# A product-gradient ring, an earlier load list and a skewed first group in the tail of an adaLN / spectral / GLU backward kernel

## The chip, the cores and the metric

The kernel runs on one core of a Trainium2 chip. The metric is device time of one execution in microseconds (us); a set of runs is given by its median, lowest and highest. A profiled execution has a time of its own and a span, from the first recorded instruction to the last. The engines are TensorE (PE, matrix products; its weight loads are PEld), VectorE (DVE), ScalarE (ACT), GpSimd (POOL) and SyncE (SP, here used only to issue DMA transfers; POOL issues some too). PE runs at a granted clock which the profile shows as a share of full speed (PEclk).

## The reference

A block of a diffusion transformer, forward and backward. The forward part, cut to what matters (S = 2048, D = 576, F = 4608, bf16):

```python
mod = (silu(c) @ w_mod).reshape(1, 6, 1, -1)
sa, ca, ga, sb, cb, gb = (mod[:, k] for k in range(6))
h = layernorm(x) * (1 + ca) + sa
x = x + ga * irfft2(rfft2(h) * (w_r + 1j * w_i))
h = layernorm(x) * (1 + cb) + sb
x = x + gb * (((h @ w_gate) * (h @ w_up)) @ w_down)
```

The function returns x and, for a given grad_out, the gradients of x, w_r, w_i, w_gate, w_up, w_down, c and w_mod: out_0 to out_8. The Fourier transforms are done as matrix products with tables. Three outputs matter here. out_0 is the forward result, whose last product is h @ w_down, the "down projection". out_8, the gradient of w_mod [576, 3456], is an outer product: for each of the six sections of 576 columns (one for each of sa, ca, ga, sb, cb, gb), silu(c) as a column times the section's gradient as a row. out_7, the gradient of c, needs for each of the 576 rows of w_mod the sum over all columns of w_mod times the same gradients.

## The kernel before, in words

The kernel computes the gradients of the GLU first, in stages that fill most of the span. The part that the change touches is its tail, from L976, the last 285 us or so. It has two kinds of work for PE.

One is three staged pipelines over the 16 row tiles (128 rows each) or 8 pairs of columns. Stage 1 (t1_norm, t1_out, t1_turn, t1_last) is the backward pass of the second layer norm and the first transform along the columns; its tile gx is written to DRAM by POOL (L1223, one store for each tile t). Stage 2 (t2_cols, t2_rows, t2_filter, t2_back) goes through the spectral filter; its products b_GY, fm, sd are made by DVE and used by PE, sd at L256. Stage 3 (t3_cols, t3_rows, t3_norm, t3_sums) transforms back and ends with the first layer norm; its result ob is out_1.

The other is the down projection (L1471 to L1515), which fills PE's gaps in those pipelines. It goes over 8 pairs of row tiles (tp_). A pair's hidden values come in four tiles named hl (quarters of 9 blocks of 128, L1293), and w_down, in blocks of 128 rows, lies in six tiles named wd, loaded once (L1279): blocks from 0, 7, 14, 21 and 28 on, seven each, and block 35. For each row tile ti of the pair and half h of the columns there is a group of NFB = 36 matmuls (L1495) into one PSUM bank u3p; there are two such banks, and in the last pair banks u3q besides. In the first pair the two row tiles of one half are done together, block by block, so that both banks run side by side. When a bank is full, ACT copies it (ob, L1500), which frees the bank; with both halves there, DVE multiplies and adds twice (of, L1508 and L1509; for the last tile in halves, L1512 and L1513) and POOL stores the tile (L1514).

The order on each engine is written out by hand. `deal` (L1055) puts 24, 24 and 21 matmuls of the down projection into each step of the three stages, and fixes the order of PE, ACT and DVE; `in_order(end_sp)` fixes SP's queue at the end; `behind` puts a transfer behind a given instruction. POOL's order comes from the list at L1309: each entry names a tile t of stage 1 and the loads that are issued directly behind the store of its gx, an integer being an hl quarter and a pair (f0, n) a wd tile.

```python
for t, *loads in ((1, (0, 7)), (2, 0), (3, (7, 7)), (4, 1), (5, (14, 7)), (6, 2), (7, (21, 7), 3), (8, (28, 7), (35, 1))):
```

The six buffers of hl tiles lie in six pools, and a table at L1293 says which tile goes into which.

out_8 is made by `product_rows` (L1147): for section j and row block m (five: four of 128 rows and one of 64), ACT scales the gradient row d by silu(c) (L1152) into one slice of a tile o8 [128, 5, 576]. There is one buffer of it. With the fifth block SP issues two stores, one of four blocks (L1154) and one of the last 64 rows (L1155). Four sections (their gradients lie in the tile early) are done in stage 2, two row blocks in each of its steps, the last two (gradients in the tile ends: dca for ca, MCA, and dsar for sa, MSA) after stage 3.

The sums for out_7 are made by `section_sum` (L1161): DVE multiplies a tile of w_mod with the gradients, writes the products into a scratch tile pr and adds them up into a column of gsc, a tile that a POOL memset (L1028) has set to zero. Row blocks of the first four sections are read into tiles wmE (three buffers, so that blocks 3 and 4 are loaded again into the first two when their sums are done), the last two into wmL (four buffers, block 4 being loaded again). After the sums come gs, gcf, gcd (L1548 to L1552), two matmuls gcp (L1558), gcr and the store of out_7.

At the end SP issues, in this order: hl loads of the last pair, four loads of wmL, two stores of a part of the filter gradient (gback_d, L1523), the stores of the rows of MCA, the reloads wmE 3 and 4 (L1159), two copies in DRAM that reverse that part into out_2 and out_3 (L1539), the rows of MSA, the last wmL, out_7.

add_zero (L1102) opens the PSUM banks in which column sums grow (csA to csE), by a product of the identity with a tile of zeros.

Of the kernel before, what the change touches and what calls it, by code (L numbers as in the profile page):

```python
# [86 lines left out]
def build(ctx, tc, A_x, A_w_r, A_w_i, B_w_gate, B_w_up, B_w_down, c_in, w_mod, grad_out,  # L87
# [58 lines left out]
    def traced():  # L146
        return len(nc.cur_bb.bb.instructions)
# [828 lines left out]
    with ExitStack() as ts:  # L976
# [11 lines left out]
        tl0 = pool("tl0", 1)  # L988
        zero = tl0.tile([128, 512], BF, name="zero")
        tl = pool("tl", 1)  # L990
# [111 lines left out]
        def add_zero(*banks):  # L1102

            for cs in banks:
                nc.tensor.matmul(cs[:], lhsT=ident[:], rhs=zero[:], start=True, stop=False)

# [37 lines left out]

        o8s = {}

        def product_rows(j, m, d):  # L1147

            if m == 0:
                o8s[j] = tl.tile([128, 5, D], BF, name="o8")  # L1150
            r, o8 = RM[m], o8s[j]
            nc.scalar.activation(out=o8[r, m, :], in_=d[r, :], func=ACT.Copy, scale=sc_col[r, m:m + 1])  # L1152
            if m == 4:
                nc.sync.dma_start(out_8[0:512, j * D:(j + 1) * D].rearrange("(m q) n -> q m n", q=128), o8[:, 0:4, :])  # L1154
                nc.sync.dma_start(out_8[512:576, j * D:(j + 1) * D], o8[64:128, 4, :])  # L1155

# [4 lines left out]
        def section_sum(m, wm, d, n, k):  # L1161
            r = RM[m]
            return nc.vector.scalar_tensor_tensor(out=pr[r, 0:n * D], in0=wm[r, :], scalar=1.0, in1=d[r].rearrange("p j n -> p (j n)"), op0=MUL, op1=MUL, accum_out=gsc[r, m, k:k + 1])

# [123 lines left out]
        def hl_load(nq, eng=nc.sync, behind_=None):  # L1288
            if nq >= 28:
                hl = hlp.tile([128, 9, 256], BF, name="hl2")  # L1290
            else:
                slot[0] += 1
                hl = hlt[(0, 3, 2, 4, 1)[slot[0]] if slot[0] < 5 else (0, 3, 2, 5, 4, 1)[(slot[0] + 1) % 6]].tile([128, 9, 256], BF, name="hl")  # L1293
            queued(eng, behind_, hl[:], hhT_d[nq // 4, :, 9 * (nq % 4):9 * (nq % 4) + 9, :])
            if nq == 13:
                in_order([last[eng], ld3["gxc", "ins", 0]])
            return hl
# [10 lines left out]
        first_hl = []  # L1308
        for t, *loads in ((1, (0, 7)), (2, 0), (3, (7, 7)), (4, 1), (5, (14, 7)), (6, 2), (7, (21, 7), 3), (8, (28, 7), (35, 1))):  # L1309
            for x in loads:  # L1310
                if isinstance(x, int):
                    first_hl.append(queued_load(t, hl_load, x, nc.gpsimd))
                else:
                    queued_load(t, wd_load, *x)
# [148 lines left out]
        wme = [secp.tile([128, 4 * D], BF, name="wmE%d" % k) for k in range(3)]  # L1463
        pr = secp.tile([128, 4 * D], BF, name="pr")
        secq = pool("secq", 1, "right", stack=rA)
# [6 lines left out]
        for tp_ in range(NT // 2):  # L1472
# [10 lines left out]
            for group in [[(0, 0), (1, 0)], [(0, 1), (1, 1)]] if tp_ == 0 else [[(0, 0)], [(0, 1)], [(1, 0)], [(1, 1)]]:  # L1483
                mark = traced()
                p2 = {}
                for ti, h in group:
                    n3 = 4 * tp_ + 2 * ti + h
                    p2[ti] = ps_cs.tile([128, 512], FP32, name="u3q", tag="cs" + "AB"[n3 // 2 % 2]) if tp_ == NT // 2 - 1 and n3 % 2 else ps_u3.tile([128, 512], FP32, name="u3p")
                    if h == 0:
                        obs[ti] = o2p.tile([128, D], BF, name="ob3", bufs=4)  # L1490
                for fb in range(NFB):
                    f0, w = wd_part(fb)
                    mms = []
                    for ti, h in group:
                        mm = nc.tensor.matmul(p2[ti][:, 0:288], lhsT=hls[fb // 9][:, fb % 9, ti * 128:(ti + 1) * 128], rhs=w[:, fb - f0, h * 288:(h + 1) * 288], start=(fb == 0), stop=(fb == NFB - 1))  # L1495
                        mms.append(mm)
                for (ti, h), mm in zip(group, mms):
                    if (tp_, ti, h) == (NT // 2 - 1, 1, 1):
                        continue
                    followed(mm, nc.scalar.copy(obs[ti][:, h * 288:(h + 1) * 288], p2[ti][:, 0:288]))  # L1500
                proj += pe_since(mark)
                for ti, h in group:
                    if h == 0:
                        continue
                    t = 2 * tp_ + ti
                    of = o2p.tile([128, D], BF, name="of3", bufs=3)
                    if t < NT - 1:
# [6 lines left out]
                    nc.gpsimd.dma_start(o0_v[:, t, :], of[:])  # L1514
                then_dve[mms[-1].ins.name] = of_engine(mark, "DVE")  # L1515
        end_sp += [i_ for i_ in nc.cur_bb.bb.instructions[last_mark:] if i_.engine == mybir.EngineType.SP]
        end_pe = []
        with tc.issue_after(ld3["last"]):
# [3 lines left out]
            for c in range(2):  # L1522
                nc.sync.dma_start(gback_d[c], wn[:, c, NPR + 1:NT, 0:DF])  # L1523
            end_sp += of_engine(mark_sp, "SP")
            for at, (j, d) in zip((12, 12), ((MCA, dca), (MSA, dsar))):
                mark_pe = traced()
                spread(d)
                for m in range(5):
                    product_rows(j, m, d)
                end_pe.append((at, pe_since(mark_pe), of_engine(mark_pe, "Activation")))  # L1530
            mark = traced()
            for m in range(5):
                section_sum(m, wmE[m][0], early, 4, 0)
                if m < 2:
                    wmE.append(section_load(m + 3, MGA, 4, wme[m]))
                    end_sp.append(wmE[-1][1])
            mark_sp = traced()
            for c, o_v in enumerate((o2_v, o3_v)):
# [86 lines left out]
```

## Time and profile before

| | |
|---|---|
| three runs | 1529.7 us median, 1525.87 to 1531.91 |
| the profiled execution | 1528.03 us, its span 1526.3 us |
| mean granted clock of TensorE | 0.985 |
| busy: PEld | 987.9 us, 65% of the span |
| busy: DVE | 1047.6 us, 69% |
| busy: ACT | 559.5 us, 37% |
| busy: POOL | 233.1 us, 15% |

How to read it: a busy time is the sum over an engine's instructions, without those that only issue a transfer or wait. In a row of a timeline stand the start and the length in us, the engine, the line of the kernel, the operation, what is written and read (out<-in), shapes, how many instructions are taken together (x), and in brackets the idle time of the engine just before it with what ended it. "DMA wd<-..." there is the landing of a transfer. An instruction of SPq or POOL named DMA_DIRECT2D is the issue of a transfer; the landing comes later. The DMA share is the mean busy share of the 16 DMA engines.

### The profile page before, as it was taken

How to read it: one execution, taken by the hardware profiler on the slowest of the kernel's cores; microseconds unless marked ns; L12 is line 12 of the kernel's file. 1: busy time of each engine (PE TensorE's matmuls, PEld its weight loads, DVE VectorE, ACT ScalarE, POOL GpSimd, SP SyncE). 2: the span in 40 equal slices, each digit the busy share in tenths (PEclk: the TensorE clock that was granted, in tenths of full speed). 3: DMA queues.
4: the chain of work that ended last, by engine and by line, in shares of the span. 5: the costliest groups of instructions: out<-in, count | busy, mean ns of one | idle time of the engine just before them, and what ended most of it. 6: DMA issues, size and time to landing. Idle time of an engine off the chain costs nothing. (4 is left out here: it accounts for less than half of the span.)

```text
span 1526.3 us, 27836 instructions
## 1 busy us (share of the span) xinstructions
PE 1460.6 (96%) x10713; PEld 987.9 (65%) x10713; DVE 1047.6 (69%) x2537; ACT 559.5 (37%) x1196; POOL 233.1 (15%) x370
## 2 busy tenths in 40 slices
PE   7999999999999999999999999999999997999965
PEld 5665544666766666667666666676666675777653
DVE  7485755676766767767666777676676675497974
ACT  7566833222222222222222222222222265475541
POOL 1101211110111111112011011021110122202210
PEclk8999999999999999999999999999999999999997
DMA  9967975868776876866777687687685678836884
GB/s 336 303 192 215 241 222 157 175 137 167 171 152 126 172 150 138 156 147 152 146 154 158 132 162 162 119 172 149 132 178 111 133 208 312 286 121 186 228 245 100
DMA packets 486836, 271.12 MB, mean 178 GB/s; under 512 B 409677, under 2 KB 456910, under 8 KB 486318
## 3 DMA queue, kind: packets, MB, share of 16 engines
q1 hardware_dynamic: 459454, 170.15, 51.7%
q0 software_dynamic: 27248, 99.18, 21.9%
q8 instruction: 84, 1.38, 0.4%
q14 instruction: 50, 0.41, 0.1%
HBM read 105.14 MB, written 81.25 MB: 122 GB/s over the span
## 5 line engine op out<-in xcount | busy, mean ns | idle before, releaser
L914 DVE TENSOR_TENSOR acc<-acc,u8p 128x288 f32<-128x288 f32 (+1 forms) x1088 | 482.4, 452 | 276.7 <-PE u8p L909 272.8
L909 PE MATMUL u8p<-wT,ggT 128*128 128x288 bf16 x1152 | 327.9, 286 | 1.5 <-DVE acc L914 1.4
L909 PE MATMUL u8p<-wT,guT 128*128 128x288 bf16 x1152 | 327.6, 286 | 0.0
L870 PE MATMUL gup<-h2T,wgu 128*128 128x512 bf16 x1152 | 297.8, 379 | 0.0
L789 ACT CAST so<-u57p 128x288 bf16<-128x288 f32 x208 | 83.0, 399 | 507.2 <-PE u57p L787 507.2
L1495 PE MATMUL u3p<-wd,hl 128*128 128x288 bf16 x1080 | 152.8, 291 | 32.4 <-ACT ob L1500 22.6
L787 PE MATMUL u57p<-h2p,gg_sf 128*128 128x288 bf16 x1088 | 176.6, 286 | 0.0
L787 PE MATMUL u57p<-h2p,gu_sf 128*128 128x288 bf16 x1088 | 176.6, 286 | 0.0
L870 PEld LDWEIGHTS <-wgu 128*128 128x128 bf16 x1152 | 109.6, 98 | 97.9 <-issue 17.1
L909 PEld LDWEIGHTS <-ggT 128*128 128x128 bf16 x1152 | 112.6, 98 | 66.4 <-issue 14.0
L578 PE MATMUL u4p<-goT,wdT 128*128 128x512 bf16 x668 | 154.6, 379 | 0.8 <-ACT ghh_st L172 0.8
L1495 PEld LDWEIGHTS <-hl 128*128 128x128 bf16 x1152 | 112.6, 99 | 64.9 <-issue 32.2
L909 PEld LDWEIGHTS <-guT 128*128 128x128 bf16 x1152 | 112.7, 98 | 57.1 <-issue 2.0
L872 ACT CAST gT<-gup 128x512 bf16<-128x512 f32 x144 | 84.4, 586 | 131.4 <-PE gup L870 129.5
L787 PEld LDWEIGHTS <-hh_sf 128*128 128x128 bf16 x1152 | 112.7, 98 | 28.4
L787 PEld LDWEIGHTS <-gu_sf 128*128 128x128 bf16 x1088 | 106.5, 98 | 27.0
L787 PEld LDWEIGHTS <-gg_sf 128*128 128x128 bf16 x1088 | 106.5, 98 | 26.8
L872 ACT CAST uT<-gup 128x512 bf16<-128x512 f32 x144 | 84.4, 586 | 77.8 <-PE gup L870 77.0
L578 PEld LDWEIGHTS <-wdT 128*128 128x128 bf16 x668 | 63.6, 98 | 72.2 <-issue 6.5
L787 PE MATMUL u57p<-gonC,hh_sf 128*128 128x288 bf16 x576 | 99.7, 286 | 0.0
L885 POOL DMA_DIRECT2D hhT_d<-hhT x36 | 33.2, 923 | 373.4 <-DVE hhT L874 372.8
L172 ACT CAST ghh_st<-u4p 128x512 bf16<-128x512 f32 x102 | 58.4, 586 | 59.6 <-PE u4p L578 57.5
(270 smaller groups left out, 1694.2 us busy)
## 6 DMA issues: line engine op xcount, KB each, us to landing
hhT_d<-hhT POOLq DMA_DIRECT2D x36, 512.0 KB, 6.5
ghhT_d<-ghh_st POOLq DMA_DIRECT2D x35, 512.0 KB, 3.6
ghh<-ghhT_d POOLq DMA_DIRECT2D x35, 512.0 KB, 7.5
hl<-hhT_d SPq DMA_DIRECT2D x28, 576.0 KB, 5.6
out_dram<-woT SPq DMA_DIRECT2D x68, 128.0 KB, 2.0
wd<-in_B_w_down_dram POOLq DMA_DIRECT2D x37, 144.0 KB, 4.6
wdn<-in_B_w_down_dram SPq DMA_DIRECT2D x18, 288.0 KB, 4.7
out_dram<-so SPq DMA_DIRECT2D x36, 144.0 KB, 2.5
```

The costliest lines, as they stand in the source:

```text
L172: nc.scalar.copy(dst, src)
L578: nc.tensor.matmul(pt[:], lhsT=wdTs[k][:, j, m, :], rhs=goT[:, 4 * sb4:4 * sb4 + 4, m, :], start=(m == 0 and n == 5), stop=(m == n - 1))
L787: mm = nc.tensor.matmul(pw[0][:, 0:288], lhsT=sf[:, t, :], rhs=rhs_n(t, h * 288, 288), start=(t == 0), stop=(t == NT - 1))
L789: followed(mm, nc.scalar.copy(so[:, h * 288:(h + 1) * 288], pw[0][:, 0:288]))
L870: nc.tensor.matmul(pts[k][:], lhsT=wgu[:, 4 * wi_ + m, jw * 128:(jw + 1) * 128], rhs=h2T[:, ts_, m, :], start=False, stop=(m == 3))
L872: nc.scalar.copy((gT, uT)[wi_][:, th_, :], pts[k][:])
L885: nc.gpsimd.dma_start(hhT_d[:, :, fb, :].rearrange("tp f x -> f tp x"), hhT[:].rearrange("f (tp ti) p -> f tp (ti p)", ti=2))
L909: nc.tensor.matmul(pu[:, 0:288], lhsT=l_, rhs=r_, start=(k == 0), stop=(k == len(mms) - 1))
L914: summed[t] = nc.vector.tensor_tensor(out=ghb(t)[:, hs_] if fbs[-1] == NFB - 1 else dst, in0=dst, in1=pu[:, 0:288], op=ADD).ins
L1495: mm = nc.tensor.matmul(p2[ti][:, 0:288], lhsT=hls[fb // 9][:, fb % 9, ti * 128:(ti + 1) * 128], rhs=w[:, fb - f0, h * 288:(h + 1) * 288], ...
```

## The change

The edits are these. (1) The zero tile has 32 columns in place of 512 and is read 16 times over by add_zero. (2) product_rows takes one tile [128, 576] for each row block, from a ring of six, and issues a store for each block: 30 stores in place of 12. The five rows of MSA come from a ring of five of their own, "o8e". (3) SP's order at the end has the rows of MCA ahead of the wmE reloads, and the rows of MSA behind them, ahead of the reversing copies. (4) section_sum writes its products over the w_mod tile it reads; the scratch tile pr is gone. (5) The list of loads on POOL: wd(0), hl 0, wd(7) and wd(14) behind the store of t=1, hl 1 and 2 behind t=2, wd(21) behind t=4, wd(28) and wd(35) behind t=5, hl 3 behind t=7. The table of hl buffers is changed with it. (6) In the first pair's groups the two row tiles are no longer taken in turn block by block: the order goes by the key 2·fb + 13·ti, so that tile 0 runs six to seven blocks ahead of tile 1. (7) The tiles named of have two buffers in place of three.

```diff
-        zero = tl0.tile([128, 512], BF, name="zero")
+        zero = tl0.tile([128, 32], BF, name="zero")
...
-                nc.tensor.matmul(cs[:], lhsT=ident[:], rhs=zero[:], start=True, stop=False)
+                nc.tensor.matmul(cs[:], lhsT=ident[:], rhs=zero[:].unsqueeze(1).to_broadcast([128, 16, 32]), start=True, stop=False)
...
-        o8s = {}
-
-        def product_rows(j, m, d):
-
-            if m == 0:
-                o8s[j] = tl.tile([128, 5, D], BF, name="o8")
-            r, o8 = RM[m], o8s[j]
-            nc.scalar.activation(out=o8[r, m, :], in_=d[r, :], func=ACT.Copy, scale=sc_col[r, m:m + 1])
-            if m == 4:
-                nc.sync.dma_start(out_8[0:512, j * D:(j + 1) * D].rearrange("(m q) n -> q m n", q=128), o8[:, 0:4, :])
-                nc.sync.dma_start(out_8[512:576, j * D:(j + 1) * D], o8[64:128, 4, :])
+        def product_rows(j, m, d, pool=None):
+
+            r, r0 = RM[m], 128 * m if m < 4 else 512
+            o8 = tl.tile([128, D], BF, name="o8", bufs=6) if pool is None else pool.tile([128, D], BF, name="o8e", bufs=5)
+            nc.scalar.activation(out=o8[r, :], in_=d[r, :], func=ACT.Copy, scale=sc_col[r, m:m + 1])
+            return nc.sync.dma_start(out_8[r0:r0 + r.stop - r.start, j * D:(j + 1) * D], o8[r, :]).ins
...
-            return nc.vector.scalar_tensor_tensor(out=pr[r, 0:n * D], in0=wm[r, :], scalar=1.0, in1=d[r].rearrange("p j n -> p (j n)"), op0=MUL, op1=MUL, accum_out=gsc[r, m, k:k + 1])
+            return nc.vector.scalar_tensor_tensor(out=wm[r, :], in0=wm[r, :], scalar=1.0, in1=d[r].rearrange("p j n -> p (j n)"), op0=MUL, op1=MUL, accum_out=gsc[r, m, k:k + 1])
...
-                hl = hlt[(0, 3, 2, 4, 1)[slot[0]] if slot[0] < 5 else (0, 3, 2, 5, 4, 1)[(slot[0] + 1) % 6]].tile([128, 9, 256], BF, name="hl")
+                hl = hlt[(0, 2, 1, 3, 4)[slot[0]] if slot[0] < 5 else (0, 2, 1, 5, 3, 4)[(slot[0] + 1) % 6]].tile([128, 9, 256], BF, name="hl")
...
-        for t, *loads in ((1, (0, 7)), (2, 0), (3, (7, 7)), (4, 1), (5, (14, 7)), (6, 2), (7, (21, 7), 3), (8, (28, 7), (35, 1))):
+        for t, *loads in ((1, (0, 7), 0, (7, 7), (14, 7)), (2, 1, 2), (4, (21, 7)), (5, (28, 7), (35, 1)), (7, 3)):
...
-        pr = secp.tile([128, 4 * D], BF, name="pr")
...
-                for fb in range(NFB):
+                mms = {}
+                for fb, (ti, h) in sorted(((fb, g_) for fb in range(NFB) for g_ in group), key=lambda x: 2 * x[0] + 13 * x[1][0]):
                     f0, w = wd_part(fb)
-                    mms = []
-                    for ti, h in group:
-                        mm = nc.tensor.matmul(p2[ti][:, 0:288], lhsT=hls[fb // 9][:, fb % 9, ti * 128:(ti + 1) * 128], rhs=w[:, fb - f0, h * 288:(h + 1) * 288], start=(fb == 0), stop=(fb == NFB - 1))
-                        mms.append(mm)
-                for (ti, h), mm in zip(group, mms):
+                    mms[ti] = nc.tensor.matmul(p2[ti][:, 0:288], lhsT=hls[fb // 9][:, fb % 9, ti * 128:(ti + 1) * 128], rhs=w[:, fb - f0, h * 288:(h + 1) * 288], start=(fb == 0), stop=(fb == NFB - 1))
+                for ti, h in group:
+                    mm = mms[ti]
...
-                    of = o2p.tile([128, D], BF, name="of3", bufs=3)
+                    of = o2p.tile([128, D], BF, name="of3", bufs=2)
...
+            rows_sp = {}
             for at, (j, d) in zip((12, 12), ((MCA, dca), (MSA, dsar))):
                 mark_pe = traced()
                 spread(d)
-                for m in range(5):
-                    product_rows(j, m, d)
+                rows_sp[j] = [product_rows(j, m, d, secq if j == MSA else None) for m in range(5)]
                 end_pe.append((at, pe_since(mark_pe), of_engine(mark_pe, "Activation")))
+            end_sp += rows_sp[MCA]
...
                     end_sp.append(wmE[-1][1])
+            end_sp += rows_sp[MSA]
```

In the built program the gsc memset on POOL now waits for PE's last L821 matmul, since gsc takes memory that the stage before still reads; on POOL it stands ahead of wd(28), of the store of t=6 and of wd(35).

2 lines of the change are left out of this document (1 added, 1 removed).

## The prediction, made before the changed kernel ran

> **What bounds the kernel now.** I began with the page's busy times and slices.
>
> ```profile
> PE 1460.6 (96%) x10713; PEld 987.9 (65%) x10713; DVE 1047.6 (69%) x2537; ACT 559.5 (37%) x1196; POOL 233.1 (15%) x370
> ```
>
> TensorE (PE) is busy for 96% of the 1526.3 us span, so only its 65 idle us can be won by reordering; the change removes almost none of its work. All edits lie after 1240 us (the tail from L976), so I read only that part: what PE waited for, stretch by stretch, then the engine behind each wait. First the waits of PE between 1260 and 1300 us (total, times, longest):
>
> ```profile
> PE u3p L1495 <- DMA wd<-in_B_w_down_dram: 6.3, 2, 3.9
> PE u3p L1495 <- ACT ob L1500: 2.1, 2, 1.1
> PE u3p L1495 <- ACT wo_l L822: 1.2, 1, 1.2
> ```
>
> Here the down projection starts: its weights (wd) come too late. PE's timeline places the two waits for wd:
>
> ```profile
> 1272.18 1.04 PE L1495 MATMUL u3p<-wd,hl 128*128 128x288 bf16 x4 [3.87 <-DMA wd<-in_B_w_down_dram]
> ...
> 1278.94 3.38 PE L1495 MATMUL u3p<-wd,hl 128*128 128x288 bf16 x14 [2.45 <-DMA wd<-in_B_w_down_dram]
> ```
>
> It has one for hl (the transposed hidden tiles) later:
>
> ```profile
> 1302.70 2.50 PE L1495 MATMUL u3p<-wd,hl 128*128 128x288 bf16 x19 [1.19 <-DMA hl<-hhT_d]
> ```
>
> The stretches of this part, and one of the end (start and end, length, busy time of PE, PEld, DVE, ACT, POOL, PE's granted clock, DMA share, GB/s):
>
> ```profile
> 1240.00:1255.00 15.00, 14.54 (x168) 12.92 (x166) 10.73 (x33) 13.57 (x30) 4.02 (x7) 1.00 0.78 241
> 1270.00:1275.00 5.00, 2.82 (x24) 2.34 (x24) 0.70 (x3) 1.32 (x4) 1.41 (x2) 0.73 1.05 377
> 1275.00:1280.00 5.00, 2.55 (x15) 1.60 (x14) 2.99 (x9) 1.83 (x4) 1.07 (x2) 0.84 1.04 388
> 1280.00:1285.00 5.00, 3.91 (x31) 2.68 (x30) 0.70 (x3) 2.25 (x7) 0.00 (x0) 0.75 0.40 124
> 1485.00:1490.00 5.00, 0.00 (x0) 0.00 (x0) 0.00 (x0) 0.00 (x0) 0.00 (x0) 0.50 1.24 107
> ```
>
> While PE waits for weights the DMA engines are full (1.05), after having had room (0.78); the clock sinks to 0.73 with the waits. In the last stretch no engine computes at all. The timelines of ACT and PE say why:
>
> ```profile
> 1494.20 3.56 ACT L1152 ACTIVATE o<-ends,sc_col 128x576 bf16<-128x576 bf16 x5 [18.27 <-DMA out_dram<-o]
> ```
>
> ```profile
> 1498.24 5.90 PE L1495 MATMUL u3p<-wd,hl 128*128 128x288 bf16 x36 [20.46 <-ACT ob L1500]
> ```
>
> The second section's five rows need the single tile that the first section's stores still read; the bank copies (ob) stand behind them on ACT, and PE waits 20.46 us for a bank.
>
> **Head: earlier weights.** POOL issues these loads in the order of its queue (L1223 is the store behind which a load is placed). The store of tile t=4:
>
> ```profile
> 1252.65 0.58 POOL L1223 DMA_DIRECT2D gx_d<-gxr  x1 [1.91 <-ACT gxr L1052]
> ```
>
> The loads wd(21) and hl3, behind t=7, and wd(28) with wd(35), behind t=8:
>
> ```profile
> 1263.66 0.98 POOL L1279 DMA_DIRECT2D wd<-in_B_w_down_dram  x1
> 1264.63 0.58 POOL L1279 DMA_DIRECT2D hl<-hhT_d  x1
> ```
>
> ```profile
> 1269.87 1.54 POOL L1279 DMA_DIRECT2D wd<-in_B_w_down_dram  x2 [0.24 <-issue]
> ```
>
> In the new list wd(21) stands behind t=4: it is issued near 1253.2 instead of 1263.66, 10.4 us sooner, far more than the 3.87 it came late. wd(28) and wd(35) stand behind t=5; but the gsc memset (L1028) now stands ahead of them on POOL and waits for the last L821 matmul:
>
> ```profile
> 1260.23 0.27 PE L821 MATMUL u57p<-gu_sf,h2p 128*64 128x256 bf16 x1
> ```
>
> So they go out near 1260.7 instead of 1269.87, 9.2 sooner against 2.45. Behind the memset POOL has the stores from t=6 on, which nobody waits for before stage 2, and hl3. I count both waits gone (6.3). The clock: in the three stretches from 1270 PE worked 2.82, 2.55 and 3.91 us at 0.73, 0.84 and 0.75 of full speed; these are shorter at full clock by 0.27, 0.16 and 0.25 of each, 2.15 us.
>
> Against this stands the load hl3. It hardly moves (1264.63 to about 1263.7), but its first use, block 27, is now reached near 1268.5, since nothing stops PE before. How long such a load takes from issue to landing, by the hl tile's row on POOL:
>
> ```profile
> DMA to landing us min/median/max: 4.2/7.3/9.3
> ```
>
> That gives a stall between 0 and 4.5; from the median (1271) and the lighter queue, which has the weights out of its way by then, I take 1.0.
>
> **Skew.** Seven matmuls of bank 0 now come before bank 1's first, and bank 0 ends 6.5 blocks ahead, so its copy on ACT runs under PE's work. Seven matmuls of at most 0.16 us (36 took 5.90 in PE's last row above, after the low clock) cover up to 1.1 of the 1.2 for wo_l; at full clock I take 0.8. One ob wait of the two (1.07) goes; I count the other's 1.07 as lost to a longer hl wait at 1302.70, which it only precedes. Head: 6.3 + 0.8 + 1.07 + 2.15 − 1.0 = 9.3; by the bounds 5 (hl3 4.5 late, the clock won back by half) to 10.7 (no stall for hl3, all of wo_l covered).
>
> **Middle: ring of six.** ACT waits twice for a row store in stage 2. The first wait
>
> ```profile
> 1339.83 0.78 ACT L1152 ACTIVATE o<-early,sc_col 128x576 bf16<-128x576 bf16 x1 [2.08 <-issue]
> ```
>
> is handed on to DVE:
>
> ```profile
> 1342.60 1.56 DVE L225 TENSOR_TENSOR b_GY<-es,fq 128x292 bf16<-128x292 f32 x4 [1.66 <-ACT es L223]
> ```
>
> From there DVE works without a gap up to its sd copies:
>
> ```profile
> 1383.77 0.68 DVE L243 COPY sd<-fm 128x512 bf16<-128x512 bf16 x4
> ```
>
> The second, with the bank copies behind it on ACT, decides when PE begins L256:
>
> ```profile
> 1377.44 0.77 ACT L1152 ACTIVATE o<-early,sc_col 128x576 bf16<-128x576 bf16 x1 [3.65 <-issue]
> ```
>
> ```profile
> 1387.15 1.04 PE L256 MATMUL fq<-T_GB,sd 128*128 128x256 bf16 x8
> ```
>
> The rows of this section on ACT (duration shortest, median, longest; first and last start), and the landing of a row store by the o tile's row at the end of the kernel:
>
> ```profile
> L1152 ACT ACTIVATE o<-early,sc_col x20: 759/776/797, 1321.4 to 1386.5; 128x576 bf16<-128x576 bf16 x16, 64x576 bf16<-64x576 bf16 x4
> ```
>
> ```profile
> DMA to landing us min/median/max: 5.2/5.8/13.6
> ```
>
> Twenty rows in 65.1 us are 3.4 us apart; with six tiles a row waits for a store six rows old, 20 us back against a landing of 5.8. The first wait cost DVE 1.66, so sd is done 1.7 sooner, at 1384.4 − 1.7 = 1382.7 (the last copy's end is 1383.77 + 0.68). With the second wait gone too, that is what PE waits for. Gain 1387.15 − 1382.8 = 4.35; at least 1.7 (the first wait alone), at most 2.08 + 3.65 = 5.7. Stage 3 behind it is untouched:
>
> ```profile
> 1391.00:1470.00 79.00, 72.95 (x640) 56.83 (x639) 67.40 (x173) 45.41 (x108) 20.14 (x38) 1.00 0.82 231
> ```
>
> PE (72.95 of 79) and DVE (67.40) work there through chains that start with stage 2's results, so it hands the gain on.
>
> **End: own rows for the last section.** With five tiles of its own, the last section's rows no longer wait: ACT's five (3.56) start 18.27 sooner, at 1475.93, and PE, released by the bank copies behind them, is back 18.3 sooner, near 1480. But DVE waits for something else, a weight tile that SP issues behind the first section's rows:
>
> ```profile
> 1480.29 1.56 SPq L1154 DMA_DIRECT2D out_dram<-o  x1
> 1481.94 1.33 SPq L1155 DMA_DIRECT2D out_dram<-o  x1
> 1483.37 2.72 SPq L1159 DMA_DIRECT2D wmE<-in_w_mod_dram  x2
> ```
>
> ```profile
> 1496.28 2.56 DVE L1163 SCALAR_TENSOR_TENSOR pr<-wmE,early 128x2304 bf16<-128x2304 bf16 x1 [16.78 <-DMA wmE<-in_w_mod_dram]
> ```
>
> The change leaves the same bytes ahead of that reload, so I leave 1496.28 where it is. Sum 3 (2.56) ends at 1498.85. Behind it DVE had an output tile that waited for PE, and then sum 4:
>
> ```profile
> 1509.02 0.46 DVE L1508 TENSOR_TENSOR of<-ob,gb_h 128x576 bf16<-128x576 bf16 x1 [9.30 <-ACT ob L1500]
> 1509.51 0.46 DVE L1509 TENSOR_TENSOR of<-of,x1t 128x576 bf16<-128x576 bf16 x1
> 1510.00 2.56 DVE L1163 SCALAR_TENSOR_TENSOR pr<-wmE,early 64x2304 bf16<-64x2304 bf16 x1
> ```
>
> PE being 18.3 sooner, that tile (0.98) follows at once, and sum 4 begins at 1499.8, 10.2 sooner. Only the last reload, issued when the first wmL sum is done, can still come late. Its issue and its use:
>
> ```profile
> 1513.99 0.53 SPq L1159 DMA_DIRECT2D wmL<-in_w_mod_dram  x1
> ```
>
> ```profile
> 1518.20 1.36 DVE L1163 SCALAR_TENSOR_TENSOR pr<-wmL,ends 64x1152 bf16<-64x1152 bf16 x1
> ```
>
> The issue moves to 1503.8 with the rest; the tile was used without a wait, so it lands within 4.2; now the reversed copies, pushed back by five more stores, may share the queue with it: 0.7, between 0 and 3. End: 10.2 − 0.7 = 9.5, by bounds 7 to 11. PE's four groups (5.90 at most each) end before DVE's sums do, so PE isn't last.
>
> **Counted at nothing.** The five zero matmuls keep their shape, only the source shrinks. The sums in place write as many elements. Two hl loads of stage 2 now stand behind two row stores on SP, some 1.5 us later, and are used groups later. The ring of the tiles named of (3 to 2) adds a wait for a store at the third output tile, near 1318; DVE was idle behind it:
>
> ```profile
> 1324.77 1.56 DVE L225 TENSOR_TENSOR b_GY<-es,fq 128x292 bf16<-128x292 f32 x4 [5.52 <-ACT es L223]
> ```
>
> A store that is 1 to 2 us late fits into these 5.52; without them it would cost as much. Eighteen more issues on SP at about 1.5 us lie beside its long idle time in the middle; at the end they can put the wmE reload back by up to 4.6 (three more ahead of it), which the full queue hides; without it the end's gain is 5.
>
> A rule speaks against the whole of it. The Trainium skill, "DMA: Bandwidth & Descriptors", section "Measured (HBM→SBUF, 128 partitions, SWDGE, issued from GpSimd)", tells one to batch transfers to 1 MiB or more, since small ones are bound by descriptors; the change splits stores of 576 KB into four of 144. By that rule the splitting would cost something on each of 18 more stores; the SP rows above, a second store issued 1.65 us after the first, which was still under way, don't show stores that wait for each other. The skill's page "TensorE: Matmul & The Clock Gate", section "Part 1: The HAM clock gate", has the clock halved after an idle window of about 3.4 us; the row 1485 to 1490, at 0.50, agrees, and by that rule the first group after 1480 would run at full clock.
>
> **The sum.** 9.3 + 4.35 + 9.5 = 23.15 us. It is taken off the profiled run, 1528.0 us (span 1526.3 and 1.7 around it): 1504.9. The median of the runs shown, 1529.7, lies 1.7 above the profiled run; I keep 1505, the difference being small against the spread of those runs (1525.87 to 1531.91).
>
> **Rivals.**
> 1. The head is bound by bytes, not by issue. For: the share is already 1.05 from 1270 and the same loads must come. Against: 0.78 before 1255, where wd(21) now goes. Then the first wd wait, 3.9, goes and the rest stays, less the 1.0 of hl3: head gain 3, time 1511.
> 2. The wait in the end only moves. For: DVE's 16.78 is untouched, and three more store issues stand ahead of the reload, five ahead of the reversed copies. Then the reload comes up to 4.6 later and the last wmL reload 3 later: end gain 2, time 1512.
> 3. The ring doesn't free ACT: stores stand in SP's queue behind loads that wait, so a tile comes back as late as before. Against: 20 us of room in the middle, own tiles at the end. It takes away the middle's 4.35 and half of the end's 9.5: 1514.
> 4. Slower: the stores serialise, each waiting for the one before to land. Ten stores from 1480.3 at 5.8 (the median landing above) end at 1538, the last wmL reload lands near 1542, sums and the way out take 8 more: 1550, less the 14 won ahead of it, 1537 in all. It decides from about 4.8 us a store; the 1.65 between two issues speaks against it.
>
> **How the numbers follow.** The forecast, 1500 to 1510, has 0.60; rivals 0.15 (head), 0.12 (end moved), 0.05 (ring), 0.08 (slower). The range takes in rivals 1 and 2 and the lower ends of gains that I counted short: 1498 to 1515. About 0.5%, 7.6 us, is what a measurement of this kernel can tell from no change; Slower by that needs rival 4 (0.08); within it needs two of the first three together, which would take 15 of the 23 (0.04); the rest, 0.88, is faster.
>
> **What would show it.** Head: no wait for wd on L1495, a short one for hl near block 27, the clock near 1 from 1265 to 1285. Middle: no ACT wait on L1152, PE at L256 4 us nearer to the start of stage 2. End: ACT without its 18.27, PE's 20.46 down to about 2, DVE's wait for wmE as long as before and sum 4 right behind output 14. A wait of DVE for wmL, or the last store after 1500 ending late, would show rival 2 or 4; a wd wait of over 2 us rival 1.

## The result, and the profile after

Four runs of the changed kernel have a median of 1507.5 us (1506.0 to 1510.0), four of the kernel before beside them 1529.2 (1525.9 to 1531.9). The ratio is 0.9857, with a 95% interval of 0.9837 to 0.9878: 21.7 us faster, where 24.7 (1529.7 to 1505) had been forecast. The profiled execution took 1507.1 us, its span 1505.3.

To see where the time came from, both traces are cut at the same five instructions: the first copy of woT in ACT's timeline of this part, the spread of dgb (end of stage 1), the last eight L256 (end of stage 2), the first spread of the last gradients (end of stage 3), and DVE's last copy. The kernel before:

```profile
1238.27 0.37 ACT L822 CAST woT<-u57p 128x256 bf16<-128x256 f32 x1 [1.35 <-PE u57p L821]
1311.79 1.13 PE L1136 MATMUL spp<-dgb_l,ones_f 128*128 128x288 f32 x4
1387.15 1.04 PE L256 MATMUL fq<-T_GB,sd 128*128 128x256 bf16 x8
1470.59 0.45 PE L1136 MATMUL spp<-ends,ones_f 128*128 128x288 bf16 x2 [2.30 <-DVE ends L1122]
1522.01 0.20 DVE L1562 CAST gcr<-gcp 1x64 bf16<-1x64 f32 x1
```

The changed kernel:

```profile
1239.01 0.37 ACT L822 CAST woT<-u57p 128x256 bf16<-128x256 f32 x1 [1.35 <-PE u57p L821]
1305.42 1.13 PE L1136 MATMUL spp<-dgb_l,ones_f 128*128 128x288 f32 x4
1377.52 1.05 PE L256 MATMUL fq<-T_GB,sd 128*128 128x256 bf16 x8 [0.96 <-DVE sd L243]
1461.57 0.64 PE L1136 MATMUL spp<-ends,ones_f 128*128 128x288 bf16 x2 [2.16 <-DVE ends L1122]
1501.09 0.20 DVE L1557 CAST gcr<-gcp 1x64 bf16<-1x64 f32 x1
```

The differences of neighbouring starts, which the experiments below use as well:

| us | head | stage 2 | stage 3 | end |
|---|---|---|---|---|
| before | 73.52 | 75.36 | 83.44 | 51.42 |
| changed | 66.41 | 72.10 | 84.05 | 39.52 |
| gained | 7.11 | 3.26 | −0.61 | 11.90 |
| forecast | 9.3 | 4.35 | 0 | 9.5 |

**Head.** The waits of PE between 1235 and 1320 us:

```profile
PE u3p L1488 <- ACT wo_l L822: 4.0, 1, 4.0
PE u3p L1488 <- DMA hl<-hhT_d: 2.0, 2, 1.0
PE u57p L821 <- ACT woT L822: 0.5, 1, 0.5
PE u3p L1488 <- ACT ob L1493: 0.2, 1, 0.2
```

No wait for wd is left, and the bank copies cost 0.2 in place of 2.1. But the wait for wo_l has gone from 1.2 up to 4.0, where the prediction had some 0.4. Four timelines (POOL, DVE, ACT, PE) show how it came about:

```profile
1254.66 1.08 POOL L1274 DMA_DIRECT2D hl<-hhT_d  x2 [7.43 <-DMA x1c<-x_d]
```

```profile
1261.59 0.82 DVE L1045 SCALAR_TENSOR_TENSOR gxr<-gn,rstd2g,n2s 128x576 bf16<-128x576 bf16 x1 [3.82 <-DMA gx_d<-gxr]
```

```profile
1262.91 0.87 ACT L1052 ACTIVATE gxr<-n2s,ab 128x576 bf16<-128x576 bf16 x1 [3.50 <-DVE ab L1047]
```

```profile
1266.23 3.19 PE L1488 MATMUL u3p<-wd,hl 128*128 128x288 bf16 x15 [4.02 <-ACT wo_l L822]
```

POOL stands 7.43 us at the load of hl 1. (The page names the transfer that landed last; by the built program's order of waits this load also takes memory that a store of so still reads. That store is issued at 1244.5 and lands 9.5 us later, at 1254.0; in the kernel before, without the early wd loads ahead of it, it landed after 2.2.) Behind it on POOL are the gx stores of t=3 and t=4. The gxr tiles are a ring of four, so DVE waits 3.82 us for one of these stores; ACT waits for DVE, and the wo_l copy that frees PE's bank stands behind ACT's wait. The clock follows (a stretch of the same trace, columns as in the prediction; the wait ends 1.2 us into it):

```profile
1265.00:1270.00 5.00, 3.77 (x24) 2.75 (x23) 3.75 (x12) 2.91 (x7) 2.19 (x4) 0.69 1.00 331
```

**Middle.** ACT waits for no row store any more, and L256 is bound by sd (0.96 in the row at 1377.52), as foreseen.

**End.** SP's order of issues, and DVE's waits in it:

```profile
1460.28 2.42 SPq L1154 DMA_DIRECT2D wmL<-in_w_mod_dram  x4
1462.80 4.03 SPq L1516 DMA_DIRECT2D gback_d<-wn  x2
1466.92 5.95 SPq L1150 DMA_DIRECT2D out_dram<-o  x5
1472.96 4.58 SPq L1154 DMA_DIRECT2D wmE<-in_w_mod_dram  x2
1480.50 2.65 SPq L1150 DMA_DIRECT2D out_dram<-o8e  x5
```

```profile
DVE wmE L1158 <- DMA wmE<-in_w_mod_dram: 11.8, 1, 11.8
DVE of L1501 <- ACT ob L1493: 1.6, 1, 1.6
DVE wmL L1158 <- DMA wmL<-in_w_mod_dram: 1.4, 1, 1.4
```

ACT's 18.27 and PE's 20.46 are gone, the wait for the wmE reload is the largest one left, and output tile 14 stands ahead of sum 4 without a wait. The reload was first used at 1484.58, 23.0 us after the spread, where it was 25.7 before (1496.28 − 1470.59); against that, DVE waits 1.4 for the last wmL block.

### The profile page after: what moved, and what is told of

Read it like the earlier page. It is cut to its first block, busy times and chain, and to the rows that moved or that the text cites. A ratio compares the mean times of both kernels' runs of the same rounds, so it can differ in the third digit from the quotient of the medians.

```text
span 1505.3 us, 27865 instructions
## 1 busy us (share of the span) xinstructions
PE 1458.0 (97%) x10713; PEld 986.7 (66%) x10713; DVE 1046.8 (70%) x2537; ACT 560.1 (37%) x1196; POOL 232.7 (15%) x370
## 4 chain that ended last, share of the span: by engine, by line
PE 85%; DVE 4%; DMA 4%; issue 4%; ACT 1%; POOL 1%; SPq 1%; POOLq 0%; DVEq 0%; ACTq 0%
PE u57p L787 27%; PE u8p L909 19%; PE gup L870 17%; PE u4p L578 9%; PE u3p L1488 3%; PE gup L865 3%; PE fq L651 1%; DMA hl<-hhT_d 1%; PE fq L212 1%; PE fq L276 1%; DMA x1t<-x_d 1%; DVE gwt L1325 1%; PE fq L256 1%; DMA out_dram<-ob 1%; DMA out_dram<-so 1%
## 5 line engine op out<-in xcount | busy, mean ns | idle before, releaser
L1488 PE MATMUL u3p<-wd,hl 128*128 128x288 bf16 x1080 | 150.2, 289 | 10.1 <-DMA hl<-hhT_d 4.6
```

What stands on the lines that cost most here:

```text
L1488: mms[ti] = nc.tensor.matmul(p2[ti][:, 0:288], lhsT=hls[fb // 9][:, fb % 9, ti * 128:(ti + 1) * 128], rhs=w[:, fb - f0, h * 288:(h + 1) * ...
```

## The experiments

Each run was timed beside the kernel before (1527.3 to 1529.4 us median in the three sets). The stretches are cut as above. All traces agree on stage 3 (83.4 to 85.0).

| us | time | ratio, 95% | head | stage 2 | end |
|---|---|---|---|---|---|
| u_head | 1514.0 | 0.9900 to 0.9929 | 71.38 | 73.31 | 39.33 |
| u_skew | 1507.7 | 0.9862 to 0.9907 | 67.14 | 72.39 | 38.98 |
| u_mid | 1514.2 | 0.9893 to 0.9943 | 69.00 | 74.69 | 39.27 |
| u_own | 1519.8 | 0.9939 to 0.9971 | 69.37 | 71.91 | 48.46 |
| hl_later | 1507.8 | 0.9839 to 0.9889 | 68.33 | 71.22 | 40.23 |
| shift | 1509.1 | 0.9846 to 0.9904 | 66.76 | 74.89 | 39.56 |
| reload | 1507.2 | 0.9830 to 0.9890 | 68.95 | 73.25 | 39.03 |
| both5 | 1503.0 | 0.9812 to 0.9863 | 68.09 | 70.67 | 32.17 |
| hl3_early | 1505.0 | 0.9827 to 0.9863 | 65.56 | 73.55 | 38.97 |
| best | 1499.7 | 0.9779 to 0.9826 | 65.25 | 73.48 | 29.46 |
| d_stores | 1511.6 | 0.9865 to 0.9901 | 66.53 | 72.95 | 43.81 |
| end_alone | 1515.7 | 0.9893 to 0.9939 | 71.42 | 74.40 | 39.81 |

One thing is read from the table before anything else. Six traces have the changed kernel's head untouched (changed, u_mid, u_own, shift, reload, d_stores); their heads last 66.4 to 69.4 us. A single pair of traces can't size a part of some 5 us there. The ends of the same code (changed, u_head, u_skew, hl_later, hl3_early) lie within 39.0 to 40.2.

### u_head: the old list and no skew

```diff
-        for t, *loads in ((1, (0, 7), 0, (7, 7), (14, 7)), (2, 1, 2), (4, (21, 7)), (5, (28, 7), (35, 1)), (7, 3)):
+        for t, *loads in ((1, (0, 7)), (2, 0), (3, (7, 7)), (4, 1), (5, (14, 7)), (6, 2), (7, (21, 7), 3), (8, (28, 7), (35, 1))):
...
-    ... key=lambda x: 2 * x[0] + 13 * x[1][0]):
+    ... key=lambda x: 2 * x[0] + x[1][0]):
```

(and the old table of hl buffers)

> The changed kernel with the old list of loads, the old table of hl buffers and no skew: the rest of the change alone. Theory (the head's gain is handed on whole): from the start of the tail to the spread of dgb the two traces differ by 76.30 - 69.17 = 7.1 us, so 1507.5 + 7.1 = about 1514.6 (1513 to 1516), with the waits for wd of 6.3 back. Rival (part of the head's gain is lost again in stage 2, where the waits for hl grew from 0.9 to 2.6): about 1512.5, with the hl waits of stage 2 back at 0.9.

1514.0, the theory's number; the hl waits of stage 2 stayed long (2.4), so the rival is not borne out. The head's own stretch is 71.38, though, only 5.0 longer than in the changed kernel's trace and 3.5 longer than the mean of the six (67.8); the times differ by 6.5 (1514.0 against 1507.5). The wait for wd is back, with 4.9 of the 6.3 (PE's waits between 1255 and 1300):

```profile
PE u3p L1488 <- DMA wd<-in_B_w_down_dram: 4.9, 3, 3.1
```

### u_skew: the two banks in turn again

```diff
-    ... key=lambda x: 2 * x[0] + 13 * x[1][0]):
+    ... key=lambda x: 2 * x[0] + x[1][0]):
```

> The changed kernel with the first pair's two banks in turn again, block by block. Theory: the two waits for a bank copy (2 x 1.07) come back in place of 0.21, and the wait for wo_l grows from 4.0 by the 0.9 that seven matmuls covered: 2 to 3 us more, 1510. Rival (those waits only take over from the later ones for hl, 2.0 in all at 1292 and 1294): 1507.5, within 0.7.

1507.7: the rival. The waits of PE between 1255 and 1300 us:

```profile
PE u3p L1488 <- ACT wo_l L822: 4.8, 1, 4.8
PE u3p L1488 <- ACT ob L1493: 2.1, 2, 1.1
```

Both waits grew as the theory says, by 0.8 and 1.9, and the two for hl (2.0) are gone: PE gets to those tiles just as much later. All of PE's waits in that stretch come to 6.9, against 6.2 with the skew. No gain of the skew shows in the time.

### u_mid: the single tile back in stage 2

```diff
-            o8 = tl.tile([128, D], BF, name="o8", bufs=6) if pool is None else pool.tile([128, D], BF, name="o8e", bufs=5)
+            if pool is None:
+                if m == 0:
+                    o8s[j] = tl.tile([128, 5, D], BF, name="o8")
+                o8 = o8s[j][:, m, :]
+            else:
+                o8 = pool.tile([128, D], BF, name="o8e", bufs=5)[:]
...
+            if pool is None and j != MCA:
+                if m == 4:
+                    nc.sync.dma_start(out_8[0:512, j * D:(j + 1) * D].rearrange("(m q) n -> q m n", q=128), o8s[j][:, 0:4, :])
+                    nc.sync.dma_start(out_8[512:576, j * D:(j + 1) * D], o8s[j][64:128, 4, :])
+                return
...
-                    of = o2p.tile([128, D], BF, name="of3", bufs=2)
+                    of = o2p.tile([128, D], BF, name="of3", bufs=3)
```

> The changed kernel with the single tile of five rows and two stores a section again for the four sections in stage 2 and for the rows of MCA (these with a store each), and with three of tiles; the last section keeps its five tiles. Theory: ACT waits for a row store twice in stage 2, 2.08 and 3.65 before, and these are worth 3.2 (what was seen) to 5 us: 1510.7 to 1512.5. Rival (the middle's gain comes from the earlier start of stage 2 and not from the ring): 1507.5, with the two ACT waits there but no later L256.

1514.2, more than expected, but with runs from 1509.7 to 1523.4: in the profiled one (1523.4) the tail began 11 us late, ahead of any edit, so the time says little and the trace more. ACT's two waits are back, 2.08 as before and 3.69 in place of 3.65 (its timeline in stage 2):

```profile
1346.97 0.78 ACT L1156 ACTIVATE o<-early,sc_col 128x576 bf16<-128x576 bf16 x1 [2.08 <-issue]
...
1384.61 0.78 ACT L1156 ACTIVATE o<-early,sc_col 128x576 bf16<-128x576 bf16 x1 [3.69 <-issue]
```

Their price is best read behind the hl waits of this stage, from ACT's second pair of es copies (L223; 1332.56 before, 1327.90 changed) to the last L256. All eleven traces with the ring have 49.6 or 49.7 there. With the single tile it is 54.6 (before), 54.3 (u_mid) and 52.9 (end_alone): 3.3 to 5.0 us. (The third buffer of the tiles named of, which this run brings back too, bears on a wait ahead of that stretch.)

### u_own: no tiles of its own for the last section

```diff
-                rows_sp[j] = [product_rows(j, m, d, secq if j == MSA else None) for m in range(5)]
+                rows_sp[j] = [product_rows(j, m, d) for m in range(5)]
```

> The changed kernel with the last section's five rows in the ring of six, no tiles of their own. Theory: the second row and those after it wait for the stores of the section before, which took 10.2 to 10.9 us to land after an issue near 1467 to 1472, so ACT's rows end near 1483 instead of 1471, PE's last four groups begin near 1483, output tile 14 delays sum 4 by some 5 to 7 us: 1512 to 1515. Rival A (the DVE wait for the wmE reload, until 1484.6, hides it): 1507.5 to 1509. Rival B (stores land as late as before the change): 1517 or more.

1519.8, beyond the theory and at rival B. ACT's and PE's timelines:

```profile
1485.15 2.90 ACT L1149 ACTIVATE o<-ends,sc_col 128x576 bf16<-128x576 bf16 x4 [14.37 <-DMA out_dram<-o]
```

```profile
1488.52 7.06 PE L1488 MATMUL u3p<-wd,hl 128*128 128x288 bf16 x36 [16.71 <-ACT ob L1493]
```

The mechanism is the one foreseen and its size was not: the stores go out behind gback (from 1474.1), so the wait is 14.4 us, most of the 18.27 of the kernel before. The end is 8.9 longer than in the changed kernel. The five tiles are most of the end's gain (11.9); the rest of the end's edits together leave 3.0 of it (51.42 − 48.46).

### hl_later, then hl3_early: moving the loads that hold POOL

hl_later:

```diff
-        for t, *loads in ((1, (0, 7), 0, (7, 7), (14, 7)), (2, 1, 2), (4, (21, 7)), (5, (28, 7), (35, 1)), (7, 3)):
+        for t, *loads in ((1, (0, 7), 0, (7, 7), (14, 7)), (4, 1, 2, (21, 7)), (5, (28, 7), (35, 1)), (7, 3)):
```

> The changed kernel with hl 1 and hl 2 issued behind the store of t=4 and not of t=2. In the changed kernel POOL stood 7.43 us at hl 1, which takes memory that a store of so still reads; the gx stores of t=3 and 4 behind it came late, DVE waited 3.82 for one, ACT's wo_l copy with it, and PE 4.02 at 1266. Theory: that chain goes, the wait for wo_l falls to 0.4 or so, the clock stays up: 3 to 4.5 us less, 1503 to 1504.5. Rival (DMA is full from 1245 to 1275 and the same bytes must land): the wait turns into one for hl or wd of the same length, 1507.5 within 1.

1507.8, the rival's time, though the chain did go: the wait for wo_l fell to 0.9. PE's and POOL's timelines:

```profile
1272.87 4.47 PE L1488 MATMUL u3p<-wd,hl 128*128 128x288 bf16 x22 [3.54 <-DMA hl<-hhT_d]
```

```profile
1265.48 0.54 POOL L1274 DMA_DIRECT2D hl<-hhT_d  x1
```

PE arrived earlier and waited for hl 3, which POOL issued 7.4 us before. Order or bytes? hl3_early puts hl 3 forward:

```diff
+        for t, *loads in ((1, (0, 7), 0, (7, 7), (14, 7)), (4, 1, 2, (21, 7), 3), (5, (28, 7), (35, 1))):
...
-        nc.gpsimd.memset(gsc[:], 0.0)
...
         last[nc.gpsimd] = ld["gx", NT - 1]
+        nc.gpsimd.memset(gsc[:], 0.0)
```

> As the run before with hl 1 and 2 behind t=4, and hl 3 behind wd(21) there too, ahead of wd(28); the gsc memset goes behind all these loads. Theory (in that run the wait that the chain over POOL had caused only turned into 3.54 for hl 3, which POOL issued at 1265.5 and which landed 7 us later: a matter of the order): hl 3 goes out near 1256 and isn't waited for; a wait of about 2 for wd(28), issued near 1261, is left: 1504 to 1506. Rival (a matter of bytes: DMA is full from 1245 on): the wait goes on to wd(28) at its length, 3 or more, 1507.5 within 1.

1505.0, inside the theory's range, with an interval that overlaps the changed kernel's. The wait went on once more, to wd(28), and shrank:

```profile
1273.01 2.61 PE L1488 MATMUL u3p<-wd,hl 128*128 128x288 bf16 x20 [2.89 <-DMA wd<-in_B_w_down_dram]
```

So three orders of the same loads make PE wait 4.0, 3.5 and 2.9 us at nearly one place (in best below, with the third order again, 1.6 for wo_l and 1.0 for wd). All of PE's waits from 1255 to 1300, taken together, don't fall with them: they are 9.8 us before, 6.2 in the changed kernel, 7.9 in hl_later, 6.8 in hl3_early and 6.4 in best. The order picks the tile that is late; that the bytes set the sum, with the DMA full there (share 1.00 in the row at 1265), fits this but isn't shown. By the built program's order of waits wd(28) itself can't be issued before the last L821 matmul, whose operand lies in its memory.

### shift: the wmL tiles moved in memory

```diff
+            secq.tile([128, D], BF, name="o8e", bufs=5)
             wmL = [section_load(m, MSA, 2, secq.tile([128, 2 * D], BF, name="wmL", bufs=4)) for m in range(4)]
```

> The changed kernel with the five row tiles of the last section laid out ahead of the wmL tiles, nothing else. By the order of waits a wmL load then waits for the landing of the last out_1 store, as before the change, and SP with it. Theory (the reload of wmE landed in 8.4 us and not in 12.8 because the gback stores went out 7 us sooner, once the scratch tile was gone and the wmL tiles had moved): the gback stores go out some 6 to 7 us later, DVE waits for the reload 2 to 4.5 us longer: 1509.5 to 1512. Rival (it landed sooner because the reversed copies no longer run beside it): 1507.5 within 1.

The two landing times in that expectation belong to different tiles (8.4 is block 4's). From the issue of block 3 to its first use it is 12.9 before and 11.6 in the changed kernel, a smaller difference. SP and DVE in this run:

```profile
1462.76 8.44 SPq L1154 DMA_DIRECT2D wmL<-in_w_mod_dram  x4
1471.29 1.31 SPq L1517 DMA_DIRECT2D gback_d<-wn  x2
```

```profile
1488.67 2.56 DVE L1158 SCALAR_TENSOR_TENSOR wmE<-wmE,early 128x2304 bf16<-128x2304 bf16 x1 [13.71 <-DMA wmE<-in_w_mod_dram]
```

The gback stores went out 7.1 us after the spread (at 1464.21 here) in place of 1.2, and the reload was used 24.5 after it in place of 23.0. That doesn't settle it: in the traces that leave both the wmL tiles' place and SP's order at the end as in the changed kernel (u_head, u_skew, u_mid, hl_later, hl3_early, end_alone) the gback stores go out 2.4 to 3.6 after the spread and the reload is used 22.9 to 24.7 after it, so 24.5 lies within what the same end varies by. The end is as long as before (39.56): 1.4 more for the reload, and the 1.4 for the last wmL block gone. What makes the reload come sooner than in the kernel before stays open.

### reload, both5, best: towards a faster version

reload puts the wmE reloads ahead of the stores:

```diff
-            end_sp += of_engine(mark_sp, "SP")
+            gb_sp = of_engine(mark_sp, "SP")
+            end_sp += gb_sp[:4]
...
-            end_sp += rows_sp[MCA]
...
-            end_sp += rows_sp[MSA]
+            end_sp += gb_sp[4:] + rows_sp[MCA] + rows_sp[MSA]
```

> The changed kernel with the two wmE reloads ahead of the gback stores and of all row stores in SP's order. Theory (what is left of the end is DVE's 11.8 us for the reload, which stood in SP's queue and in the DMA queue behind stores): the reload is issued near 1466 to 1468, when the first sums are done, lands 6 to 8 later, DVE waits 2 to 4 instead of 11.8; the end comes 6 to 9 us sooner, 1499 to 1501.5. Rival (the queue is full there and the stores, now behind, make the last wmL or the reversed copies end as late): gain under 3, 1505 to 1507.5.

1507.2, the rival. The wait for the reload shrank as foreseen, from 11.8 to 2.3, and others took its place (DVE's waits from 1458 us on):

```profile
DVE of L1501 <- ACT ob L1493: 8.3, 2, 6.0
DVE wmL L1158 <- DMA wmL<-in_w_mod_dram: 3.7, 1, 3.7
DVE wmE L1158 <- DMA wmE<-in_w_mod_dram: 2.3, 1, 2.3
```

Sum 4 stands behind output tile 14 in DVE's order, which PE finishes no sooner (its first group there took 7.20 us in place of 4.57, most of it at a granted clock of 0.50 behind a wait of 3.47), and the last wmL block is issued only when the first wmL sum is done. both5 adds to reload the list of hl_later, and loads that block into the third wmE tile, ahead of the stores (tail_sp: gback and the rows):

```diff
-                    wmL.append(section_load(4, MSA, 2, secq.tile([128, 2 * D], BF, name="wmL", bufs=4)))
...
+            wmL.append(section_load(4, MSA, 2, wme[2][:, 0:2 * D]))
+            end_sp += [wmL[-1][1]] + tail_sp
```

> hl 1 and 2 behind t=4, the wmE reloads first, and the last wmL block loaded early into the third wmE tile when its sum is done. Theory: the gains add up, 3 to 4.5 in the head, 6 to 9 at the reload and 1.4 for the last wmL wait: 1493 to 1497. Rival (PE's last groups, which end near 1489 in the changed kernel, or the stores at the end become the bound): 1497 to 1500.

1503.0, a smaller gain than either had it. The end is 7.4 shorter (32.17) and still has a wait of 3.1 for output tile 14. best takes the list of hl3_early, and all sums ahead of that tile:

```diff
-            cuts = (0, 4, 10, len(sections))
+            cuts = (0, 10, 10, len(sections))
```

> The kernel with the reloads first and the last wmL block early (1503.0), with that list of loads, and with DVE doing all sums ahead of output tile 14. Theory: DVE waited 5.1 for ob before sum 4 there; with the sums first these end some 3 to 4 sooner and the end becomes PE's last group and the stores, a gain of 2 to 3; the head gives 2 to 3 if the first theory of the list holds: 1497.5 to 1500. Rival (the stores at the end and PE's last groups end it already): 1501 to 1503.

1499.7, in the theory's range, and its interval (0.9779 to 0.9826) lies clear of the changed kernel's (0.9837 to 0.9878). DVE's waits from 1458 us on are now short, and one of them is for PE's last group:

```profile
DVE wmE L1157 <- DMA wmE<-in_w_mod_dram: 1.8, 1, 1.8
DVE of L1505 <- PE u3q L1488: 1.8, 1, 1.8
DVE of L1501 <- ACT ob L1493: 1.4, 1, 1.4
```

### d_stores: twice as many stores

```diff
-            return nc.sync.dma_start(out_8[r0:r0 + r.stop - r.start, j * D:(j + 1) * D], o8[r, :]).ins
+            return [nc.sync.dma_start(out_8[r0:r0 + r.stop - r.start, j * D + k:j * D + k + 288], o8[r, k:k + 288]).ins for k in (0, 288)]
```

> The changed kernel with every row block stored in two halves of 288 columns: 60 stores in place of 30, the same bytes. Theory (a store costs its issue on SP, 0.4 to 1.2 us, and doesn't wait for the one before): nothing in stage 2; at the end five more issues ahead of the wmE reload put it 2 to 4 us back: 1508 to 1512. Rival (stores wait for each other's landing, 4.5 us or more): twenty in a row at the end take 90 us, over 1535.

1511.6, the theory's number. Stage 2, with twenty more stores, is 72.95 (72.10 in the changed kernel, 70.7 to 74.9 in the other traces with the ring). The end is 4.3 longer. SP's timeline shows the wmE reload issued 19.3 us after the spread (at 1462.09 here) in place of 11.4; it was used only 1.2 later than in the changed kernel, though, 24.2 after the spread. The other 3.1 are DVE's longer wait for the last wmL block:

```profile
1468.97 12.36 SPq L1150 DMA_DIRECT2D out_dram<-o  x10
1481.42 1.14 SPq L1154 DMA_DIRECT2D wmE<-in_w_mod_dram  x2
```

```profile
1502.09 1.35 DVE L1158 SCALAR_TENSOR_TENSOR wmL<-wmL,ends 64x1152 bf16<-64x1152 bf16 x1 [4.54 <-DMA wmL<-in_w_mod_dram]
```

Ten stores held SP for 12.4 us here, and that counts only where a load that is waited for stands behind them. They don't wait for the store just before, but the theory left out that they can wait for one further back (last section).

### end_alone: the end's part on the kernel before

The edits of u_head and of u_mid together (the small zero tile stays).

> The kernel before with the end's part of the change alone (a store for each row of the last two sections, five tiles of their own for the last one, sums in place); single tile in stage 2, old list, no skew, three of tiles. Theory (from the last section's spread to the last DVE operation the trace shows 51.4 us before and 39.5 after, so the end is worth 11.9 by itself): 1529.2 - 11.9 = 1517.3, 1516 to 1519. Rival (the end's gain needs the earlier parts, because the wait for the wmE reload is set by what runs beside it): 1521 or more.

1515.7, a gain of 13.7 on its set's 1529.4 (ratio 0.9893 to 0.9939, so 9 to 16), with an end of 39.81: the end's gain doesn't need the rest.

## Why the prediction held, and where it didn't

The time lies in the range and 2.5 above the forecast. In the profiled run the parts gained 7.1, 3.3 and 11.9 us, where 9.3, 4.35 and 9.5 had been put: errors of both signs, which nearly cancel. That the sum came so close is in part luck.

**Head, forecast 9.3.** The profiled run shows 7.1, and over several traces it is less: the three heads with the old list (73.52, 71.38, 71.42) have a mean of 72.1, the six with the new one 67.8, so 4.3; the times of u_head and the changed kernel differ by 6.5. Whichever is taken, 9.3 was too much. Both wd waits (6.3) went, and wd(21) and wd(28) were issued in time. The step that failed is the sentence "Behind the memset POOL has the stores from t=6 on, which nobody waits for before stage 2". It looked behind the memset only and not behind hl 1, whose wait is new in that place, and it forgot that DVE needs the gx stores for its ring of four gxr tiles. The wait for wo_l, 1.2 before, went to 4.0 in place of 0.4. The skew's 0.8 + 1.07 was counted as a gain and doesn't show as one (u_skew); the forecast said of the second ob wait that it would become a wait for hl, and that holds for both, and for wo_l's 0.8. The stall for hl 3, put at 1.0 with 0 to 4.5 around it, didn't show, because PE was late by more; with that lateness gone it was 3.5 (hl_later). So rival 1 was half right: the wait that is left moves on from tile to tile with the order, and the sum of the waits stays at 6 to 8 us with the new lists.

**Middle, forecast 4.35.** Both ACT waits are gone, and L256 waits for sd, as the prediction had it. Cut behind the hl waits the single tile costs 3.3 to 5.0 (u_mid). The whole stage gained 3.3 in the profiled run, since the hl waits early in it grew from 0.9 to 2.6. They belong to loads issued ahead of the row stores, and lie between 0.5 and 1.6 with the single tile and 1.2 and 4.1 with the ring; whether the ring has a part in that stays open.

**End, forecast 9.5.** The chain ran as laid out: rows at once, PE back 18 us sooner, tile 14 ahead of sum 4 without a wait. u_own puts 8.9 on the tiles of their own. The sentence that was mis-sized is "so I leave 1496.28 where it is": the reload came 2.7 sooner in this trace, and 1.0 to 2.8 sooner in the seven with this end; why stays open (shift). The last wmL block cost 1.4, against 0.7 forecast.

**Counted at nothing.** The second buffer less for the of tiles showed where it was expected, as a wait of 3.15 us for a store, and DVE still had 1.48 us idle behind it:

```profile
1315.96 0.46 DVE L1501 TENSOR_TENSOR of<-ob,gb_h 128x576 bf16<-128x576 bf16 x1 [3.15 <-DMA out_dram<-of]
...
1318.39 1.56 DVE L225 TENSOR_TENSOR b_GY<-es,fq 128x292 bf16<-128x292 f32 x4 [1.48 <-ACT es L223]
```

So it was covered, with less to spare than thought: the wait was put at 1 to 2. The zero tile and the sums in place weren't tried by themselves.

**The other rivals.** Rival 2's late reload didn't come in the changed kernel, and d_stores shows that a later issue needn't make it late: 8 us more in SP's queue put it back by 1.2. Rival 4 is refuted: with sixty stores the time is 4 us longer, where serial stores would have made it tens of us. (Its sum is a little off as well: 1550 less 14 is 1536, not 1537.) The rule of the Trainium skill against small transfers, "DMA: Bandwidth & Descriptors", section "Measured (HBM→SBUF, 128 partitions, SWDGE, issued from GpSimd)", would put a price on each of these stores. Its figures are for loads, and it calls transfers under 64 KB descriptor-bound, where most of these have 144 KB (72 in d_stores). The runs show no such price in stage 2 beyond the spread of the traces, and at the end the 4.3 us of d_stores, where loads stand behind the stores.

## What to carry to other kernels

When a load is moved up in an in-order queue, ask what it will wait for in its new place, and follow everything behind it, stores too: a store frees a buffer that some engine needs. When one wait is removed, look for the next one behind it in the same engine's order before its length is counted as a gain; here an earlier reload alone shortened the end by 0.5 us (reload), with the last wmL block early too by 7.4 (both5), and with the sums taken out from behind an output tile by 10.1 (best). And take a part of a few microseconds from several traces: untouched code varied by 3 us from one trace to the next.

## What the runs showed of the hardware that was not expected

Stores issued in a row don't wait for the one before, but in the built program each issue on SP waits for the landing of the eighth transfer before it. In d_stores the first and the ninth of the ten stores of half rows at the end are these in SP's timeline:

```profile
1468.97 2.94 SPq L1150 DMA_DIRECT2D out_dram<-o  x1
...
1480.18 0.50 SPq L1150 DMA_DIRECT2D out_dram<-o  x1
```

and from issue to landing the first took

```profile
DMA to landing us min/median/max: 11.2/11.2/11.2
```

so it landed at 1480.1, just before the ninth went out. In the changed kernel the second wmE reload went out at 1477.02 in the same way, when the first gback store, issued at 1462.80, had landed after 14.2. The number of stores thus has a price where landings are long, in the loads that stand behind them on SP. In stage 2 landings had a median of 2.8 us and an issue one of 0.34. Not all of SP's time at the end is this wait: of the five row stores of the changed kernel the first held SP for 3.54 us, the others for 0.40 to 0.65 each, and what held the first stays open.

After 4.0 us of waiting (1262.2 to 1266.2) PE's granted clock in the changed kernel was 0.50 in the three stretches of 1 us from 1267 on, and 1.00 again from 1271; until 1266 it had been 1.00. In hl3_early a wait of 2.89 left the clock at 1.00, but in u_head one of 3.13, which ended at 1276.35 and had one of 1.20 shortly before it, was followed by 0.50 (the stretch from 1275 to 1280). "TensorE: Matmul & The Clock Gate" of the Trainium skill, section "Part 1: The HAM clock gate", gives an idle window of about 3.4 us before the clock is halved. The wait of 4.0 agrees with that; the one of 3.13 shows that a single wait can be shorter and the clock still falls. The prediction had expected no such idle time to be left in the head.
